# Layer 1's last sums and splits, products of zeros at the start, and one transpose for shared last tokens

## The chip, the cores and the metric

The kernel runs on one core of a Trainium2 chip. The metric is the device time of one execution in microseconds (us), lower is better. The engines are named as in the profile: PE is the matrix engine (PEld its weight loads), DVE the vector engine, ACT the scalar engine, POOL a general engine, SP the queue that issues most transfers (DMAs). Each engine works through its own instructions in order; they wait for one another by semaphores. PE writes to PSUM, which has eight banks of 512 columns in float32 per partition.

## The reference

Attention over 4 batches of 12 heads (448 tokens, 64 columns per head) with a sigmoid in the place of a softmax, then two gated layers over the 1792 tokens, each 768 to 2048 to 768, all in float32:

```python
scores = scale * np.matmul(q, k.transpose(0, 1, 3, 2)) - np.log(S)
attn = 1.0 / (1.0 + np.exp(-scores))
attn_out = np.matmul(attn, v)
...
x = np.ascontiguousarray(attn_out.transpose(0, 2, 1, 3)).reshape(B * S, H * D)
h = x @ w_in
g = h - np.tanh(h)
x = g @ w_out
...
h = x @ w_in2
r = np.maximum(h, 0.0)
g = s * (r * r) + b
out = g @ w_out2
```

## The kernel before

The two batches of a pair go through everything together: attention of 12 head pairs, layer 1, layer 2, then the next two batches (`for sb`, lines 449 to 471). A float32 product shows as two records of `MATMUL` in the trace; products of the two layers are done in three passes on split numbers (`mm3`, line 180): a high part rounded to a shorter type, and a low part that is the rest. `split` (line 186) makes them: ACT casts the high part, DVE subtracts for the low part.

**Attention.** For head pair `i`, `prep(i)` transposes queries and keys on PE into the PSUM tile `tqk`: three blocks of 128 tokens of the queries (`rawq`), three of the keys (`rawk`). The last 64 tokens of both lie together in one tile `rawr`, the queries' in one half of the partitions and the keys' in the other. Before, `rawr` is transposed twice, once beside the queries and once beside the keys, so a head pair has eight transposes. ACT copies the queries to `qt`, DVE the keys to `kt`. `qk` makes scores (`sc`, two heads side by side, two records each) and ACT the sigmoid (`af`); `av` multiplies with the values (`o`). PE's order is transposes of pair i+1, scores of chunks 2 and 3 of pair i, chunks 0 and 1 of pair i+1, then `av`. Loads of pair i+3 are issued on SP while pair i is worked on; at the start, the keys of pairs 0 and 1 go by ACT's queue (line 202).

**Layers.** `hidden` (line 296) makes 128 rows of `h` in two blocks of tokens (512 and 384 columns) and turns them into `g`. Four of these are followed by the products with `w_out`: `y` in layer 1, 24 products for each of six row blocks (`hd` 0 and 1, `d` 0 to 2), 144 in a group, four groups a layer. After a row block, `evict` (line 350) adds its two PSUM blocks to `y` on DVE; in the last group it also makes `x2`, the split input of layer 2. `bank` (line 88) hands out five single PSUM places in turn, so a block takes the place of the block five before it and waits until that was read.

**Weights.** In the first pass over the weights (sb 0) each chunk is loaded raw as float64 words (`w_load`), converted (`w_conv`: `wy` on ACT, then `wa`, `wa`, `wf` on DVE, and a store to scratch) and split (`w_split`: `whi` on ACT, `wlo` on DVE). In the second pass (sb 1) the float32 scratch is loaded, and only the split is left. `w_ahead(n)` brings loads up to n+5, conversions up to n+3 and splits up to n+2; line 372 and line 378 call it after `evict(0)` and `evict(1)`. What stands in an engine's queue is in the order in which these Python lines run.

Of the kernel before, what the change touches and what calls it, by code (L numbers as in the profile page):

```python
# [9 lines left out]
F32 = mybir.dt.float32  # L10
# [3 lines left out]
ALU = mybir.AluOpType  # L14
# [5 lines left out]
def tile_kernel(ctx, tc, q, k, v, w_in1, w_out1, w_in2, w_out2, s_in, b_in, out):  # L20
# [62 lines left out]
    def banks(name):  # L83
        return ps_p.tile([P, 2, 512], F32, tag="two", name=name, bufs=3)
# [77 lines left out]
    def upto(step, n):  # L162

        while done[step] <= n:
            yield from step(done[step]) or ()
            done[step] += 1

    def w_ahead(n, parts="ab"):

        if "a" in parts:  # L170
            yield from upto(w_load, n + 5)
            yield from upto(w_conv, n + 3)
        if "b" in parts:
            yield from upto(w_split, n + 2)

    def now(g):
        for _ in g:
# [8 lines left out]
    def split(hi, lo, t):  # L186
        act.copy(hi, t)
        dve.tensor_tensor(out=lo, in0=t, in1=hi.bitcast(F32), op=ALU.subtract)
# [4 lines left out]
    def qkv_load(i, what="qkv"):  # L193
        if i >= B * NP:
            return
        b, hs = i // NP, slice(i % NP * 2, i % NP * 2 + 2)
        if "q" in what:
            raws[i] = {"r": at_p.tile([P, 2, D], F32, tag="rawr", name="rawr", bufs=4)}
        for nm in what:
            src = {"q": q, "k": k, "v": v}[nm]  # L200

            dma = act if i < 2 and nm == "k" else sp
            rest = src[b, hs, SM:S, :].rearrange("h p d -> p h d")
            if nm == "v":
                t = at_p.tile([P, 2, NJ + 1, D], F32, tag="rawv", name="rawv", bufs=4)

                o = RM * (b % 2)
                pool.memset(t[RM - o:P - o, :, NJ, :], 0.0)
                tt, last = t[:, :, 0:NJ, :], t[o:o + RM, :, NJ, :]
                dma.dma_start(out=tt.rearrange("p e j d -> p e (j d)"), in_=src[b, hs, 0:SM, :].rearrange("h (p j) d -> p h (j d)", p=P))  # L210
            else:
                t = at_p.tile([P, NJ, 2, D], F32, tag=f"raw{nm}", name=f"raw{nm}", bufs=4)

                o = RM * ((nm == "k") ^ (b % 2))
                last = raws[i]["r"][o:o + RM]
                for e in range(2):
                    dma.dma_start(out=t[:, :, e, :], in_=src[b, hs.start + e, 0:SM, :].rearrange("(p j) d -> p j d", p=P))
            dma.dma_start(out=last, in_=rest)
            raws[i][nm] = t

    def prep(i):

        if i >= B * NP:
            return
        b = i // NP
        rq, rk, rr = (raws[i][nm] for nm in "qkr")
        both = banks("tqk")

        def transpose(ps, r, first):

            o = 0 if first else SM
            pe.transpose(ps[:, o:o + P], rr.rearrange("p h d -> p (h d)"), ident)
            for j in range(NJ):
                o = (j + first) * P
                pe.transpose(ps[:, o:o + P], r[:, j].rearrange("p h d -> p (h d)"), ident)
            return ps[:, RM:RM + S] if first else ps[:, 0:S]

        qt = at_p.tile([P, S], F32, tag="qt", name="qt", bufs=2)
        kt = at_p.tile([P, S], F32, tag="kt", name="kt", bufs=2)
        tq, tk = transpose(both[:, 0], rq, b % 2), transpose(both[:, 1], rk, 1 - b % 2)  # L240
        act.copy(qt, tq)
        dve.tensor_copy(kt, tk)
        ready[i] = qt, kt
        avs[i] = []
# [85 lines left out]
    def layer1(sb, order):  # L330
# [3 lines left out]
        for grp in range(FC // FG):  # L334
            g = [hidden(0, x, f, order if grp == 0 and f == 0 else None) for f in range(FG)]
            for hd in range(2):
# [13 lines left out]
                def evict(d):  # L350
                    dm = hd * 3 + d
                    if grp == 0:
                        y_t[dm] = x_p.tile([P, T2], F32, tag="y", name="y", bufs=7)
                    y = y_t[dm]
                    if grp == FC // FG - 1:
                        x2.append(x_p.tile([P, 2, T2], F32R, tag="x", name="x2", bufs=CC))
                    for i, ns in enumerate(BLOCKS):
                        if grp == 0:
                            act.copy(y[:, ns], ps[d, i])
                            continue  # L360
                        dve.tensor_tensor(out=y[:, ns], in0=ps[d, i], in1=y[:, ns], op=ALU.add)
                        if grp == FC // FG - 1:
                            split(x2[dm][:, 0, ns], x2[dm][:, 1, ns], y[:, ns])

                if hd == 0:

# [2 lines left out]
                else:  # L369
                    products((0,), range(FG))  # L370
                evict(0)
                now(w_ahead(pos[0] - 2))
                if hd == 0:
                    products((1,), [FG - 1])
                else:
                    products((1,), range(FG))
                evict(1)
                now(w_ahead(pos[0] - 1))
                products((2,), range(FG))
                evict(2)  # L380
        return x2
# [50 lines left out]
                        now(w_ahead(pos[0] - 2 + t // 3))  # L432


    qkv_load(0, "qk")
    qkv_load(1, "qk")
    qkv_load(0, "v")
    qkv_load(2, "qk")
    qkv_load(1, "v")
    qkv_load(2, "v")  # L440
    sp.dma_start(out=s_sb, in_=s_in.to_broadcast([P, 1]))
    sp.dma_start(out=b_sb, in_=b_in.to_broadcast([P, 1]))

    dve.memset(nlogs, NLOGS)

    act.activation(warm, nlogs, AF.Sigmoid)
# [55 lines left out]
```

## Time and profile before

| | us |
|---|---|
| median of 3 runs | 1134.53 (1134.43 to 1134.8) |
| the profiled execution | 1135.0 |
| its span | 1133.2 |
| PE busy in the span | 1119.3 |
| DVE busy | 549.1 |
| ACT busy | 489.1 |
| POOL busy | 5.4 |

PE's "busy" is time in which a matmul was under way, not time at full pace: two matmuls overlap, so pace is read from starts, or from how long a stage with a known number of products takes. PEclk is the share of the full clock of 2.4 GHz that was granted; it has two levels, 1.00 and 0.50. The clock's records begin some 14 us into the span, and the views print 1.00 ahead of that, so at the start the level is read from the matmuls' pace.

### The profile page before, as it was taken

The numbers are of one execution on the slowest core, as the hardware profiler recorded it, in microseconds if no ns is written. First come the engines' busy times: TensorE is split into PE (matmuls) and PEld (weight loads), VectorE is DVE, ScalarE is ACT, GpSimd is POOL, SyncE is SP. The second block draws the span as 40 slices with busy tenths as digits, with TensorE's granted clock in tenths as the row PEclk, the third lists the DMA queues.
The fourth block names the chain that finished last, engine by engine and source line by source line (L and its number), as shares of the span: only waits on it lengthen the run. The fifth ranks groups of instructions, "written<-read, shape, count | busy, mean of one in ns | idle before, by whom it ended". The sixth has DMA issues, their size and how long they took to land.

```text
span 1133.2 us, 14385 instructions
## 1 busy us (share of the span) xinstructions
PE 1119.3 (99%) x5760; PEld 943.6 (83%) x5760; DVE 549.1 (48%) x805; ACT 489.1 (43%) x734; POOL 5.4 (0%) x30
## 2 busy tenths in 40 slices
PE   7999999999989999999999999999999999999998
PEld 3446889898878989999954468888889899999998
DVE  0233657767677658676621123243434541534343
ACT  4774544242436664545346643331313363516060
POOL 0000000000000000000000000000000000000000
PEclk9999999999989999999999999999999999999999
DMA  5664454545444645454444202121111111111102
GB/s 133 175 177 107 156 190 140 178 156 168 145 146 134 202 140 184 138 181 153 160 121 100 77 14 70 42 70 43 56 51 47 56 56 57 57 56 56 56 14 98
DMA packets 111970, 123.62 MB, mean 109 GB/s; under 512 B 53024, under 2 KB 87328, under 8 KB 111904
## 3 DMA queue, kind: packets, MB, share of 16 engines
q1 hardware_dynamic: 110016, 122.25, 35.7%
q8 instruction: 45, 0.74, 0.3%
q10 hardware_dynamic: 1888, 0.46, 0.2%
q14 instruction: 21, 0.17, 0.1%
HBM read 92.01 MB, written 30.67 MB: 108 GB/s over the span
## 4 chain that ended last, share of the span: by engine, by line
PE 97%; DVE 2%; ACT 1%; DMA 0%; SPq 0%; issue 0%; DVEq 0%
PE h L79 41%; PE z L79 21%; PE y L79 19%; PE sc L79 7%; PE o L79 7%; PE tqk L79 2%; ACT x L79 0%; DVE y L79 0%; DVE x L79 0%; DVE wlo L79 0%; DVE wa L79 0%; DMA rawr<-in_q_dram 0%; DVE wf L79 0%; SPq L79 0%; ACT whi L79 0%
## 5 line engine op out<-in xcount | busy, mean ns | idle before, releaser
L79 PE MATMUL h<-x,whi 128*128 128x512 f32 (+1 forms) x1536 | 434.1, 363 | 0.0
L79 PEld LDWEIGHTS h<-x,whi 128*128 128x128 f32 x1536 | 283.4, 188 | 34.9 <-issue 2.7
L79 PE MATMUL h<-x,wlo 128*128 128x512 f32 (+1 forms) x768 | 279.7, 364 | 0.0
L79 PE MATMUL z<-whi,g 128*128 128x384 f32 x896 | 229.4, 334 | 0.0
L79 PE MATMUL y<-g,whi 128*128 128x512 f32 (+1 forms) x768 | 220.4, 368 | 2.0 <-ACT whi L79 1.9
L79 ACT ACTIVATE t<-h 128x512 f32<-128x512 f32 (+1 forms) x128 | 69.6, 544 | 236.5 <-PE h L79 235.9
L79 PEld LDWEIGHTS z<-whi,g 128*128 128x128 f32 x896 | 162.0, 188 | 1.3 <-issue 1.3
L79 PEld LDWEIGHTS y<-g,whi 128*128 128x128 f32 x768 | 143.8, 189 | 19.9 <-ACT whi L79 2.2
L79 PEld LDWEIGHTS h<-x,wlo 128*128 128x128 f32 x768 | 144.1, 188 | 15.2
L79 PE MATMUL z<-wlo,g 128*128 128x384 f32 x448 | 149.7, 334 | 0.0
L79 ACT CAST whi<-wf 128x768 fp32r<-128x768 f32 x128 | 106.0, 832 | 97.7 <-DVE wf L79 53.8
L79 DVE TENSOR_TENSOR wlo<-wf,whi 128x768 fp32r<-128x768 f32 x128 | 122.0, 953 | 52.9 <-ACT whi L79 52.9
L79 PE MATMUL y<-g,wlo 128*128 128x512 f32 (+1 forms) x384 | 142.2, 370 | 1.9 <-DVE wlo L79 1.7
L79 DVE TENSOR_TENSOR g<-t,g 128x512 fp32r<-128x512 f32 (+1 forms) x128 | 79.9, 624 | 83.5 <-ACT g L79 83.5
L79 ACT ACTIVATE af<-sc,nlogs 128x896 f32<-128x896 f32 x96 | 89.1, 1008 | 23.6 <-PE sc L79 13.7
L79 ACT CAST g<-t 128x512 fp32r<-128x512 f32 (+1 forms) x128 | 72.6, 567 | 33.2 <-DVE t L79 30.9
L79 PEld LDWEIGHTS z<-wlo,g 128*128 128x128 f32 x448 | 84.1, 188 | 0.0
L79 PE MATMUL sc<-qt,kt 64*128 64x448 f32 x384 | 81.3, 561 | 1.3 <-DVE kt L79 1.3
L79 PEld LDWEIGHTS y<-g,wlo 128*128 128x128 f32 x384 | 72.8, 190 | 11.7 <-DVE wlo L79 3.2
L79 DVE TENSOR_TENSOR t<-h,t 128x512 f32<-128x512 f32 x64 | 39.9, 623 | 87.7 <-ACT t L79 87.7
L79 DVE TENSOR_TENSOR z<-z 128x384 f32<-128x384 f32 x84 | 45.2, 555 | 67.5 <-PE z L79 67.5
L79 PE MATMUL o<-af,rawv 128*64 128x448 f32 x384 | 77.5, 545 | 0.0
(33 smaller groups left out, 588.5 us busy)
## 6 DMA issues: line engine op xcount, KB each, us to landing
raw<-in_moe_w_in_dram SPq DMA_DIRECT2D x32, 768.0 KB, 5.1
raw<-in_moe_w_out_dram SPq DMA_DIRECT2D x32, 768.0 KB, 4.8
win<-wf SPq DMA_DIRECT2D x32, 384.0 KB, 2.6
wout<-wf SPq DMA_DIRECT2D x32, 384.0 KB, 2.7
wf<-win SPq DMA_DIRECT2D x32, 384.0 KB, 3.0
wf<-wout SPq DMA_DIRECT2D x32, 384.0 KB, 3.1
rawq<-in_q_dram SPq DMA_DIRECT2D x48, 96.0 KB, 2.8
rawv<-in_v_dram SPq DMA_DIRECT2D x24, 192.0 KB, 2.7
```

What stands on the lines that cost most here:

```text
L79: return lambda *a, **kw: tc.keep_in_program_order(getattr(self.engine, name)(*a, **kw))
```

## The change

In `evict`, the two sums come first, then the two casts, then the two subtractions; `w_ahead` moved into `evict` (for `d` 0 and 1), with the order of its parts turned ("ba": splits ahead of conversions, after the loads), and in the last group its first step, the cast `whi`, is put between the casts and the subtractions of `x2`. At the start, DVE clears a tile `zero` and PE multiplies it with itself twice. `prep` for pairs above 0 puts queries, shared last tokens and keys side by side in one stretch of two banks, so that one transpose of `rawr` serves both, as PE's last of the pair; for pair 0 it takes two single banks and keeps both transposes of `rawr`, at the end. The keys of pair 1 are loaded by SP, and SP's first loads stand in another order.

```diff
-        if "a" in parts:
-            yield from upto(w_load, n + 5)
-            yield from upto(w_conv, n + 3)
-        if "b" in parts:
-            yield from upto(w_split, n + 2)
+        yield from upto(w_load, n + 5)
+        for part in parts:
+            if part == "a":
+                yield from upto(w_conv, n + 3)
+            else:
+                yield from upto(w_split, n + 2)
...
-            dma = act if i < 2 and nm == "k" else sp
+            dma = act if i == 0 and nm == "k" else sp
...
+        if i:
+            flat = both.rearrange("p a b -> p (a b)")
+            parts = [(flat, 0), (flat, SM + P), (flat, SM)]
+        else:
+            one = [ps_p.tile([P, 512], F32, tag="one", name="tqk0", bufs=2) for _ in range(2)]
+            parts = [(one[0], 0), (one[1], P), (one[0], SM), (one[1], 0)]
+        for (ps, o), r in zip(parts, (rk, rq) if b % 2 else (rq, rk)):
+            for j in range(NJ):
+                pe.transpose(ps[:, o + j * P:o + (j + 1) * P], r[:, j].rearrange("p h d -> p (h d)"), ident)
+        for ps, o in parts[2:]:
             pe.transpose(ps[:, o:o + P], rr.rearrange("p h d -> p (h d)"), ident)
...
-                        dve.tensor_tensor(out=y[:, ns], in0=ps[d, i], in1=y[:, ns], op=ALU.add)
-                        if grp == FC // FG - 1:
-                            split(x2[dm][:, 0, ns], x2[dm][:, 1, ns], y[:, ns])
+                        else:
+                            dve.tensor_tensor(out=y[:, ns], in0=ps[d, i], in1=y[:, ns], op=ALU.add)
+                    fill = w_ahead(pos[0] - 2 + d, "ba") if d < 2 else iter(())
+                    if grp == FC // FG - 1:
+                        for i, ns in enumerate(BLOCKS):
+                            act.copy(x2[dm][:, 0, ns], y[:, ns])
+                        next(fill, None)
+                        for i, ns in enumerate(BLOCKS):
+                            dve.tensor_tensor(out=x2[dm][:, 1, ns], in0=y[:, ns], in1=x2[dm][:, 0, ns].bitcast(F32), op=ALU.subtract)
+                    now(fill)
...
-                now(w_ahead(pos[0] - 2))
...
-                now(w_ahead(pos[0] - 1))
...
+    zero = const.tile([P, S], F32, name="zero")
+    dve.memset(zero, 0.0)
+    for _ in range(2):
+        pe.matmul(banks("none")[:, 0, :S], zero[:, :P], zero, start=True, stop=True)
```

What the change moves, at three places. DVE in sb 0, last group of layer 1, the row block `hd` 0, `d` 0 and the sums of the next one (`y` out of PSUM, `x2` the low part, `wa`, `wf` the conversion, `wlo` a weight's low part), before:

```order
L79 TENSOR_TENSOR y_1151<-y_2587,y_1151 128x512
L79 TENSOR_TENSOR x2_2633<-y_1151,x2_2633 128x512
L79 TENSOR_TENSOR y_1151<-y_2588,y_1151 128x384
L79 TENSOR_TENSOR x2_2633<-y_1151,x2_2633 128x384
L79 TENSOR_SCALAR wa_2642<-raw_2479 128x768
L79 SCALAR_TENSOR_TENSOR wa_2642<-wy_2643,wa_2642 128x768
L79 SCALAR_TENSOR_TENSOR wf_2644<-wy_2643,wa_2642 128x768
L79 TENSOR_TENSOR wlo_2652<-wf_2580,whi_2651 128x768
L79 TENSOR_TENSOR y_1175<-y_2607,y_1175 128x512
```

The same place of the changed kernel:

```order
L79 TENSOR_TENSOR y_1147<-y_2583,y_1147 128x512
L79 TENSOR_TENSOR y_1147<-y_2584,y_1147 128x384
L79 TENSOR_TENSOR x2_2629<-y_1147,x2_2629 128x512
L79 TENSOR_TENSOR x2_2629<-y_1147,x2_2629 128x384
L79 TENSOR_TENSOR wlo_2637<-wf_2576,whi_2636 128x768
L79 TENSOR_SCALAR wa_2642<-raw_2475 128x768
L79 SCALAR_TENSOR_TENSOR wa_2642<-wy_2643,wa_2642 128x768
L79 SCALAR_TENSOR_TENSOR wf_2644<-wy_2643,wa_2642 128x768
L79 TENSOR_TENSOR y_1171<-y_2603,y_1171 128x512
```

The second sum moved ahead of the first subtraction, and `wlo` ahead of the conversion of the next chunk.

PE at the start (`tqk` the transposes of a pair, `sc` scores), before:

```order
L79 MATMUL tqk_130<-ident_78,rawr_83 128x128
L79 MATMUL tqk_130<-ident_78,rawq_84 128x128 x3
L79 MATMUL tqk_130<-ident_78,rawr_83 128x128
L79 MATMUL tqk_130<-ident_78,rawk_88 128x128 x3
L79 MATMUL sc_143<-qt_131,kt_132 128x448 x2
L79 MATMUL sc_148<-qt_131,kt_132 128x448 x2
L79 MATMUL tqk_165<-ident_78,rawr_92 128x128
L79 MATMUL tqk_165<-ident_78,rawq_93 128x128 x3
L79 MATMUL tqk_165<-ident_78,rawr_92 128x128
L79 MATMUL tqk_165<-ident_78,rawk_97 128x128 x3
```

PE at the start of the changed kernel:

```order
L79 MATMUL none_126<-zero_124 128x448
L79 MATMUL none_128<-zero_124 128x448
L79 MATMUL tqk0_136<-ident_78,rawq_84 128x128 x3
L79 MATMUL tqk0_137<-ident_78,rawk_88 128x128 x3
L79 MATMUL tqk0_136<-ident_78,rawr_83 128x128
L79 MATMUL tqk0_137<-ident_78,rawr_83 128x128
L79 MATMUL sc_150<-qt_146,kt_147 128x448 x2
L79 MATMUL sc_155<-qt_146,kt_147 128x448 x2
L79 MATMUL tqk_172<-ident_78,rawq_93 128x128 x3
L79 MATMUL tqk_172<-ident_78,rawk_97 128x128 x3
L79 MATMUL tqk_172<-ident_78,rawr_92 128x128
```

Two products of zeros stand ahead, `rawr` is transposed last, and from pair 1 on once.

SP's first loads, before:

```order
L79 DMA rawq_84<-in_q_dram 128x3x64 x2
L79 DMA rawr_83<-in_q_dram 64x2x64
L79 DMA rawq_93<-in_q_dram 128x3x64 x2
L79 DMA rawr_92<-in_q_dram 64x2x64
L79 DMA rawv_101<-in_v_dram 128x2x192
L79 DMA rawv_101<-in_v_dram 64x2x64
L79 DMA rawq_106<-in_q_dram 128x3x64 x2
```

And of the changed kernel:

```order
L79 DMA rawq_84<-in_q_dram 128x3x64 x2
L79 DMA rawr_83<-in_q_dram 64x2x64
L79 DMA rawq_93<-in_q_dram 128x3x64 x2
L79 DMA rawr_92<-in_q_dram 64x2x64
L79 DMA rawk_97<-in_k_dram 128x3x64 x2
L79 DMA rawr_92<-in_k_dram 64x2x64
L79 DMA rawv_101<-in_v_dram 128x2x192
L79 DMA rawv_101<-in_v_dram 64x2x64
```

The three loads of pair 1's keys are SP's now, ahead of the values.

## Rows read from the trace of the kernel before

**Rows 1.** The page, part 1: busy us, share of the span, instructions.
```profile
PE 1119.3 (99%) x5760; PEld 943.6 (83%) x5760; DVE 549.1 (48%) x805; ACT 489.1 (43%) x734; POOL 5.4 (0%) x30
```
**Rows 2.** Windows, three y groups, tile y: length, PE, PEld, DVE, ACT, PEclk, DMA.
```profile
245.21:274.57 29.36, 29.36 (x144) 25.99 (x144) 6.09 (x11) 0.00 (x0) 1.00 0.54 171
303.64:340.37 36.73, 32.94 (x144) 27.90 (x144) 11.94 (x20) 5.66 (x10) 0.91 0.41 129
867.11:896.81 29.70, 29.62 (x144) 25.90 (x144) 11.93 (x20) 5.67 (x10) 1.00 0.13 40
```
**Rows 3.** Timeline, DVE, last y group of sb 0: start, us, instruction, [idle before].
```profile
318.86 0.68 DVE L79 TENSOR_TENSOR y<-y 128x512 f32<-128x512 f32 x1
320.23 0.69 DVE L79 TENSOR_TENSOR x<-y,x 128x512 fp32r<-128x512 f32 x1 [0.69 <-ACT x L79]
320.85 0.55 DVE L79 TENSOR_TENSOR y<-y 128x384 f32<-128x384 f32 x1
321.97 0.56 DVE L79 TENSOR_TENSOR x<-y,x 128x384 fp32r<-128x384 f32 x1 [0.58 <-ACT x L79]
...
324.97 0.95 DVE L79 TENSOR_TENSOR wlo<-wf,whi 128x768 fp32r<-128x768 f32 x1
325.84 0.69 DVE L79 TENSOR_TENSOR y<-y 128x512 f32<-128x512 f32 x1
...
329.43 0.68 DVE L79 TENSOR_TENSOR y<-y 128x512 f32<-128x512 f32 x1
```
**Rows 4.** Timeline, ACT, the same stretch.
```profile
322.65 0.81 ACT L79 CAST whi<-wf 128x768 fp32r<-128x768 f32 x1
```
**Rows 5.** Timeline, PE, the same stretch.
```profile
323.52 0.73 PE L79 MATMUL y<-g,whi 128*128 128x512 f32 x2 [1.89 <-ACT whi L79]
...
325.98 0.79 PE L79 MATMUL y<-g,wlo 128*128 128x512 f32 x1 [1.73 <-DVE wlo L79]
```
**Rows 6.** Windows of 1 us: PE, PEld, DVE, ACT, POOL, PEclk, DMA.
```profile
324.00:325.00 1.00, 0.25 (x2) 0.00 (x0) 0.96 (x3) 0.00 (x0) 0.00 (x0) 0.86 0.03 8
...
331.00:332.00 1.00, 1.00 (x5) 0.93 (x4) 0.96 (x2) 0.01 (x1) 0.00 (x0) 0.73 0.00 0
```
**Rows 7.** Timeline, PE, a head pair in the steady part of attention.
```profile
27.78 0.49 PE L79 MATMUL tqk<-ident,rawq 128*128 128x128 f32 x3
28.11 0.27 PE L79 MATMUL tqk<-ident,rawr 128*128 128x128 f32 x1
...
28.64 3.28 PE L79 MATMUL sc<-qt,kt 64*128 64x448 f32 x16
...
35.00 0.33 PE L79 MATMUL tqk<-ident,rawr 128*128 128x128 f32 x1
```
**Rows 8.** Timeline, PE, the start.
```profile
5.26 0.45 PE L79 MATMUL tqk<-ident,rawr 128*128 128x128 f32 x1 [5.26 <-DMA rawr<-in_q_dram]
...
6.14 0.42 PE L79 MATMUL tqk<-ident,rawr 128*128 128x128 f32 x1
...
8.48 3.36 PE L79 MATMUL sc<-qt,kt 64*128 64x448 f32 x8 [1.28 <-DVE kt L79]
...
13.66 3.47 PE L79 MATMUL sc<-qt,kt 64*128 64x448 f32 x16
...
20.22 0.33 PE L79 MATMUL tqk<-ident,rawr 128*128 128x128 f32 x1
```
**Rows 9.** Timeline, DVE, the start.
```profile
0.81 0.06 DVE L79 MEMSET nlogs<- 128x1 f32 x1 [0.81 <-PEq L486]
7.80 0.62 DVE L79 COPY kt<-tqk 128x448 f32<-128x448 f32 x1 [6.93 <-ACT qt L79]
```
**Rows 10.** Timeline, SP's queue, the start: when it issues.
```profile
0.74 1.59 SPq L79 DMA_DIRECT2D rawq<-in_q_dram  x2
...
3.05 1.29 SPq L79 DMA_DIRECT2D rawq<-in_q_dram  x2
```
**Rows 11.** DMA issues up to 16 us: KB each, median us to landing.
```profile
rawq<-in_q_dram SPq DMA_DIRECT2D x8, 96.0 KB, 3.0
```

More of the change, by code (lines that the diff above doesn't have):

```diff
@@ L226, in prep @@
         rq, rk, rr = (raws[i][nm] for nm in "qkr")
-        both = banks("tqk")
-        def transpose(ps, r, first):
-            o = 0 if first else SM
+        both = banks("tqk") if i else None
+        if i:
[8 more added lines that the diff above has]
+        for ps, o in parts[2:]:
             pe.transpose(ps[:, o:o + P], rr.rearrange("p h d -> p (h d)"), ident)
[L233 to L236, printed above, removed]
+        tq, tk = (flat[:, 0:S], flat[:, S:2 * S]) if i else (one[0][:, 0:S], one[1][:, RM:P + SM])
+        if b % 2:
+            tq, tk = tk, tq
         qt = at_p.tile([P, S], F32, tag="qt", name="qt", bufs=2)
         kt = at_p.tile([P, S], F32, tag="kt", name="kt", bufs=2)
-        tq, tk = transpose(both[:, 0], rq, b % 2), transpose(both[:, 1], rk, 1 - b % 2)
         act.copy(qt, tq)
@@ L359, in evict @@
                             act.copy(y[:, ns], ps[d, i])
-                            continue
-                        dve.tensor_tensor(out=y[:, ns], in0=ps[d, i], in1=y[:, ns], op=ALU.add)
-                        if grp == FC // FG - 1:
-                            split(x2[dm][:, 0, ns], x2[dm][:, 1, ns], y[:, ns])
+                        else:
[8 more added lines that the diff above has]
+                    now(fill)
                 if hd == 0:
@@ L432, in layer2 @@
                         now(w_ahead(pos[0] - 2 + t // 3))
[L435 to L440, printed above, removed]
+    for i, what in ((0, "qk"), (1, "qk"), (0, "v"), (1, "v"), (2, "qkv")):
+        qkv_load(i, what)
     sp.dma_start(out=s_sb, in_=s_in.to_broadcast([P, 1]))
     sp.dma_start(out=b_sb, in_=b_in.to_broadcast([P, 1]))
+    zero = const.tile([P, S], F32, name="zero")
+    dve.memset(zero, 0.0)
+    for _ in range(2):
+        pe.matmul(banks("none")[:, 0, :S], zero[:, :P], zero, start=True, stop=True)
     dve.memset(nlogs, NLOGS)
```

## The prediction, as it was put on record

> **What bounds the kernel now.** I read the page first: PE is busy for 99% of the span and DVE for 48% [rows 1], so what is worth something is either PE work taken out, or PE time that is spent waiting or at half clock. The busy share hides the second, so I next laid PE's starts in a row by stage and looked for stages with the same products and another length. All stages of a kind agree within 0.05 us, with four exceptions, and the change touches three: the start, and the last group of y products in layer 1 in either pass over the weights. The fourth, the end of the span, stays as it is. A group of 144 y products takes 29.36 us where nothing waits; the last one of sb 0 takes 36.73, at a mean clock of 0.91, the last one of sb 1 29.70 [rows 2]. That is 7.37 and 0.34 us to be had.
>
> Why sb 0's is long is seen on DVE. Per row block it adds the first block, waits 0.69 us for ACT's cast of it, subtracts, adds the second, waits 0.58, subtracts, then converts and splits a chunk of weights [rows 3]. From one such step to the next it is 325.84 - 318.86 = 6.98 us; a step without weights is 329.43 - 325.84 = 3.59 [rows 3]. PE makes a row block in 29.36 / 6 = 4.89. DVE's steps are longer than PE's, four of six hold weights, and a weight's low part is the last thing in a step. PE stood for 1.89 us for a `whi`, which ACT began at 322.65 [rows 4], and for 1.73 for its `wlo` [rows 5]. After that the granted clock fell from 1.00 to 0.50 (2.4 to 1.2 GHz): the share of 0.86 in the microsecond from 324 puts the fall at 324.7, that of 0.73 from 331 the rise at 331.5 [rows 6]. From 326.0 on PE worked 5.5 us at half pace, so 2.7 of the 7.37 us are the clock's, and 4.6 to 4.7 are waits.
>
> **Term 1: one transpose less.** In the steady part three transposes are followed by the next after 28.11 - 27.78 = 0.33 us [rows 7], 0.11 each. 23 pairs lose one; pair 1's is counted with the start, so 22 x 0.11 = 2.4 us. It is on the path, as PE works through a pair without a gap: ACT and DVE are done with copies and sigmoids earlier, and their order within a pair is the same. Nothing else is late next: SP needs less than a pair's time for a pair's eight issues at 0.65 each [rows 10], 5.2 of about 7.3 us. Bounds: 1.9 (if the switch from `rawr` to another tile costs what it cost before) and 2.6.
>
> The Trainium skill, page TensorE: Matmul & The Clock Gate, Part 4: PE-mode transpose, gives about 275 ns for a transpose of 128 x 128 in a kernel. By it this term would be an estimated 22 x 0.275 = 6 us. The trace speaks against it: the busy time of one record is near that figure, but starts are 0.11 apart, and the stream's length goes by starts.
>
> **Term 2: the last group of layer 1.** In the new order the second sum no longer stands behind the first subtraction. In a step that begins at 0, by the durations of [rows 3]: sums at 0 and 0.62; ACT casts from 0.73 to 1.35 and on to about 1.8; DVE subtracts at 1.4 and 2.0; `wlo` needs ACT's `whi`, about 1.75 to 2.55, and starts at 2.6 for 0.95; the conversion, three operations, takes the rest. Of the two waits (0.69 + 0.58 = 1.27) some 0.3 is left, so a step is 1.0 us shorter: 5.95 with weights, about 2.5 without. `wlo` is ready 3.5 us into a step where it was at 6.98. DVE's first sum of the group comes 8.2 us in (7 of 24 stretches of 1.22, less the last half); its steps then end at 14.2, 20.1, 22.6, 28.5, 34.4 and 36.9. PE would need the second `wlo` of the second half at 17.6 (12 stretches for the first half, 2 more, and the high passes) and gets it at 17.7: 0.1 to 0.5 of a wait. The second block of the fifth row block takes the place of the first block of the third, which is read at 20.1 to 20.8, and PE is there at 20.1 to 20.4: 0.4 to 0.7. And layer 2's first `h` wants the last low part at 36.4 and gets it at 36.5 to 36.9: 0.15 to 0.4. Together 0.65, up to 1.5. None is near the 1.7 us waits ahead of which the clock fell; the 0.34 us in sb 1's group left it at 1.00 [rows 2]. So 7.37 - 0.65 = 6.7 us, bounds 5.4 and 7.3. What is late next is DVE still, as 5.95 stands against 4.89. The conversion comes later within a step, which nobody waits for soon: its `wf` is split one step later. In groups 0 to 2 the turned order moves nothing on PE, since they had no waits to lose. `whi` waits for PE to be done with the weights four back; those are the ones of the half before, read to the end some 4.9 us earlier, so ACT isn't held.
>
> In sb 1 steps with weights have no conversion; the wait of 0.34 us is for a `wlo` that now comes earlier. I take all of it: 0.3, bounds 0 and 0.34.
>
> **Term 3: the start.** PE begins at 5.26 and its first scores at 8.48; the transposes are 0.22 apart ((6.14 - 5.26) / 4), twice the steady 0.11, and eight score records are busy for 3.36 us, where sixteen take 3.28 later: half clock, although the view prints 1.00 there. The 16 score records from 13.66 run mostly at full pace, so the clock rose near 14.1 [rows 7, 8]. What the change does, in order. (a) DVE clears `zero` from 0.81 on. The trace has no such memset; a memset of one column is 0.06 and a copy of 448 columns out of PSUM 0.62 [rows 9], so 0.06 to 0.62, and I take 0.35. (b) The first scores, eight records, are two chunks of two heads side by side and are busy for 3.36 at half clock [rows 8], so a chunk is 1.5 to 1.7. A zero product needs all rows of the array for the same 448 columns, so it takes as long as a chunk, and both 3.0 to 3.4: from 1.2 to about 4.3. That is ahead of the data: the second query load is issued about 1.5 and lands 3.0 later, at 4.5 [rows 10, 11]. So the products hide in PE's wait; were the memset 0.6 longer, they would begin to delay. (c) Queries come first, keys next, `rawr` last, so PE can begin at about 4.6 rather than 5.26. (d) Eight transposes at half pace take 1.76, and the copies of pair 0 no longer follow each other: DVE's waited for ACT's [rows 9], and now both read banks of their own, which saves one copy of 0.5 to 0.6. Scores then start at 4.6 + 1.76 + 0.2 + 0.62 + 0.06 = 7.25, 1.2 us earlier. (e) The clock. It rose 5.6 us after the first score (8.48 to 14.1), and 5.5 us after work went on at 326.0 [rows 5, 6]. Counted from 1.2 that would be 6.8, before the scores, with everything from 7.25 on at full pace: eight score records 1.6, seven transposes 0.9, sixteen records 3.2, and the values' products 3.16 (35.00 - 28.64 - 3.2, [rows 7]) make 8.9, where 20.22 - 8.48 = 11.74 stand now. That is 2.85 (pair 1's transpose in it), 4.05 with (d). At full pace ACT's two sigmoids and a copy between the first scores and pair 1's `kt` have little room, and I leave 0.3 to 0.4 for that: 3.7. Ends: a rise at 14.1 as before leaves the earlier start and the transpose, 1.4; a rise ahead of the transposes gives another 0.85, 4.9.
>
> (f) Three loads move from ACT's queue to SP's and stand ahead of the values. They are SP's seventh to ninth issue, 0.65 each [rows 10], so the last goes out near 6.2 and lands by 9.2; pair 1's last transposes come at 7.25 + 1.6 + 0.65 = 9.5. Cover 0.3 us; without it up to 0.5 is lost, and that is in the bounds. The Trainium skill (its first page, Trainium Kernel Development and Optimization, Key Constraints) says that several issuing engines only save sequencer time, since they share 16 DMA engines. By that the move costs three issues on SP, an estimated 2 us for all that is queued behind; by the rows pair 2's last load, SP's 19th issue, goes out at 12.4, lands by 15.4 and is wanted near 16.8, so the sum stays.
>
> **Sum.** 2.4 + 6.7 + 0.3 + 3.7 = 13.1 us off. The profiled execution has 1135.0 us, 0.5 above the median of 1134.53, and 1.8 beyond its span that the change doesn't touch. Against the median: 1121.4.
>
> **Rivals.** *The clock at the start rises late.* For it: the zero products are followed by a pause until the loads land, and by another for the copies; in the trace work with pauses took 8.8 us from the first transpose to the rise. Then scores run at half pace up to about 10.5, and term 3 is 2.3 or, with no help at all, 1.4: 1122.8 to 1123.7. *DVE stays the bound in layer 1.* If a step is only 0.5 us shorter (the casts and `whi` in ACT's order hold the subtractions), PE waits 1 to 2 us twice, and the clock may fall once more for 2.7: term 2 is 2 to 4 us, 1124 to 1126. Against it: ACT's two casts and `whi` are some 2 us of a step of 6. *The change doesn't do what it says in layer 1:* the waits are for weights, and if `whi` waits as long for its `wf` as before, term 2 is 0 and the time 1128. Against it: in either order `wf` is a whole step old by then. *Slower:* the clock isn't granted in attention for long, since short waits of PE for SP's longer queue break up its work in the first pairs. A pair at half pace costs some 6 us more; 9.4 us of other gains and the 2.3 that make a difference as well as the 1.4 of the earlier start are eaten when the rise comes later than about 14 + 2 x 13 = 40 us, four pairs in: 1136.8 there, 1139.8 at 46. Against it: one transpose less makes no pause, and SP gains 2 us on PE in each pair.
>
> **How the numbers follow.** Forecast 0.60, around 1121.4 (1119.5 to 1122.7); late clock 0.22; DVE's bound 0.11; no gain in layer 1 0.04; slower 0.02; 0.01 for a sum that comes to nothing. 0.2% is 2.3 us, about the least that a measurement of this kernel tells from none. The range from 1119.5 to 1124.3 takes in the forecast with the ends of terms 1 and 3, the late clock, and the near end of DVE's bound. Faster 0.97, same 0.01, slower 0.02.
>
> **What would show it.** Seven transposes a pair and pairs 0.11 us shorter; the last y group of sb 0 near 30 us with PEclk 1.00, no idle PE over 0.8 us, and DVE's steps near 5.95; sb 1's at 29.36; two zero products ending ahead of 4.5, scores from about 7.25 with eight records in 1.6 us, and pair 2's transposes at 16.5 rather than 20.22. It is wrong if the zero products end after the first loads, if score records are at half pace past 10 us, or if a y group of sb 0 still has a window at PEclk 0.50.

## The result, and the profile after

The changed kernel takes 1122.02 us in the median beside 1134.53; the ratio is 0.9891, 95% interval 0.9879 to 0.9904. The prediction was 1121.4 in 1119.5 to 1124.3. One of the five executions, the profiled one, took 2251.33 us: its matrix products ran at about half pace from end to end, while DVE and ACT were busy for 560 and 496 us, near the usual 549 and 488, and it is left out of the ratio. What follows is read from another execution of the same program (`e1_after`, 1122.69 us median, ratio 0.9891 again, 0.9877 to 0.9904), whose span is 1120.9 us beside 1133.2 before.

The page, part 1 (busy us, share of the span, instructions), answers to [rows 1]:

```profile
PE 1114.8 (99%) x5741; PEld 939.0 (84%) x5741; DVE 549.1 (49%) x806; ACT 487.6 (44%) x734; POOL 5.4 (0%) x30
```

PE has 19 instructions fewer: 23 transposes taken out and four records of the two products of zeros put in. It is 4.5 us less busy, though 12.3 us are gone: most of the gain was idle time, or busy time at half clock that the shares don't show as loss.

**Layer 1.** Windows over three y groups, tile y (columns as in [rows 2]):

```profile
240.88:270.24 29.36, 29.36 (x144) 25.99 (x144) 6.08 (x11) 0.00 (x0) 1.00 0.53 162
299.31:329.34 30.03, 29.87 (x144) 25.86 (x144) 10.51 (x19) 4.99 (x10) 1.00 0.42 128
855.12:884.48 29.36, 29.36 (x144) 26.00 (x144) 11.89 (x21) 5.18 (x10) 1.00 0.16 44
```

The last group of sb 0 is 0.67 us longer than one that waits for nothing, where it was 7.37 longer [rows 2], and the clock of its window is 1.00. The last one of sb 1 is level. The timeline of DVE in the second of them (start, us, instruction, idle before in brackets) shows a step of the new order, which answers to [rows 3]:

```profile
313.48 1.15 DVE L79 TENSOR_TENSOR y<-y 128x512 f32<-128x512 f32 x2
314.85 1.16 DVE L79 TENSOR_TENSOR x<-y,x 128x512 fp32r<-128x512 f32 x2 [0.22 <-ACT x L79]
316.00 0.96 DVE L79 TENSOR_TENSOR wlo<-wf,whi 128x768 fp32r<-128x768 f32 x1
316.87 0.55 DVE L79 TENSOR_SCALAR wa<-raw 128x768 uint32<-128x768 uint32 x1
317.53 0.96 DVE L79 SCALAR_TENSOR_TENSOR wa<-wy,wa 128x768 uint32<-128x768 uint32 x1
318.52 0.96 DVE L79 SCALAR_TENSOR_TENSOR wf<-wy,wa 128x768 uint32<-128x768 uint32 x1
319.40 1.15 DVE L79 TENSOR_TENSOR y<-y 128x512 f32<-128x512 f32 x2
...
321.85 1.15 DVE L79 TENSOR_TENSOR y<-y 128x512 f32<-128x512 f32 x2
```

Both sums come first, both subtractions next, then the low part of a weight, then a conversion. One wait of 0.22 us for ACT is left where 0.69 and 0.58 stood. A step with weights takes 319.40 - 313.48 = 5.92 us, one without 321.85 - 319.40 = 2.45. The timeline of PE has the three places where it still stands:

```profile
317.01 0.50 PE L79 MATMUL y<-g,wlo 128*128 128x512 f32 x1
...
320.14 0.62 PE L79 MATMUL y<-g,whi 128*128 128x384 f32 x2 [0.16 <-DVE y L79]
...
335.40 0.92 PE L79 MATMUL h<-x,whi 128*128 128x512 f32 x2
```

The first begins when `wlo` (316.00 and 0.96 long) is done. Held against the starts in the group before, it and the start behind it come 0.11 and 0.10 later than the pace allows. The second waits for its bank, read by the sums of 319.40; it costs 0.31 + 0.11 = 0.42. In the third, layer 2's first `h`, the pair of records takes 0.92 instead of 0.63: it meets the low part that DVE subtracts from 335.07 on. That `h` group takes 29.38 us beside 29.09 before.

**The start.** Timeline of PE, which answers to [rows 8]:

```profile
1.39 3.35 PE L79 MATMUL none<-zero 128*128 128x448 f32 x4 [1.39 <-DVE nlogs L79]
5.02 0.87 PE L79 MATMUL tqk<-ident,rawq 128*128 128x128 f32 x3 [0.27 <-DMA rawq<-in_q_dram]
...
7.77 1.77 PE L79 MATMUL sc<-qt,kt 64*128 64x448 f32 x8 [0.81 <-DVE kt L79]
9.47 0.55 PE L79 MATMUL tqk<-ident,rawq 128*128 128x128 f32 x3
...
10.39 3.28 PE L79 MATMUL sc<-qt,kt 64*128 64x448 f32 x16
...
16.75 0.55 PE L79 MATMUL tqk<-ident,rawq 128*128 128x128 f32 x3
```

The products of zeros are over at 4.74, 0.27 us ahead of the first queries. The eight score records are busy for 1.77 us where they took 3.36, so they run at 2.4 GHz from the first on. Pair 2's transposes begin at 16.75, 3.47 us earlier than before. The timelines of DVE and ACT in the same stretch:

```profile
0.91 0.43 DVE L79 MEMSET zero<- 128x448 f32 x1 [0.91 <-PEq L499]
...
7.00 0.62 DVE L79 COPY kt<-tqk 128x448 f32<-128x448 f32 x1 [5.65 <-PE tqk L79]
```
```profile
6.78 0.53 ACT L79 COPY qt<-tqk 128x448 f32<-128x448 f32 x1 [2.51 <-PE tqk L79]
```

The copy of the keys no longer waits for ACT's, as it did in [rows 9]; the two overlap.

**A head pair in the steady part.** Timeline of PE, which answers to [rows 7]:

```profile
24.04 0.55 PE L79 MATMUL tqk<-ident,rawq 128*128 128x128 f32 x3
...
24.95 3.28 PE L79 MATMUL sc<-qt,kt 64*128 64x448 f32 x16
...
31.32 0.55 PE L79 MATMUL tqk<-ident,rawq 128*128 128x128 f32 x3
```

Seven transposes take 24.95 - 24.04 = 0.91 us from the first start to the scores, and the pair 31.32 - 24.04 = 7.28.

**The account.** By stages of PE, span against span: the start 3.47; 22 pairs with 7 transposes at 0.91 us instead of 8 at 1.02, 2.36 in all; the last y group 6.70; the `h` group behind it -0.29; sb 1's y group 0.34; one pair's scores at 54 us, 0.25 longer than before, -0.25; small ones -0.08. That is 12.25 of 12.3.

### The profile page after: what moved, and what is told of

It is laid out like the page before. It is cut to its first block, busy times and chain, and to the rows that moved or that the text cites. A ratio compares the mean times of both kernels' runs of the same rounds, so it can differ in the third digit from the quotient of the medians.

```text
span 2249.5 us, 14347 instructions
## 1 busy us (share of the span) xinstructions
PE 2243.8 (100%) x5741; PEld 1542.2 (69%) x5741; DVE 560.4 (25%) x806; ACT 495.6 (22%) x734; POOL 5.4 (0%) x30
## 4 chain that ended last, share of the span: by engine, by line
PE 100%; DVE 0%; issue 0%
PE h L79 42%; PE y L79 21%; PE z L79 21%; PE sc L79 7%; PE o L79 7%; PE tqk L79 2%; PE none L79 0%; DVE kt L79 0%; DVE z L79 0%; DVE zero L79 0%; DVE nlogs L79 0%
## 5 line engine op out<-in xcount | busy, mean ns | idle before, releaser
L79 PE MATMUL h<-x,whi 128*128 128x512 f32 (+1 forms) x1536 | 786.0, 615 | 0.0
L79 PEld LDWEIGHTS h<-x,whi 128*128 128x128 f32 x1536 | 459.0, 300 | 174.1 <-issue 150.7
L79 PE MATMUL h<-x,wlo 128*128 128x512 f32 (+1 forms) x768 | 473.8, 617 | 0.0
L79 PE MATMUL z<-whi,g 128*128 128x384 f32 x896 | 410.0, 557 | 0.0
L79 PE MATMUL y<-g,whi 128*128 128x512 f32 (+1 forms) x768 | 393.1, 615 | 0.0
L79 PEld LDWEIGHTS z<-whi,g 128*128 128x128 f32 x896 | 269.7, 302 | 50.0 <-issue 34.8
L79 PEld LDWEIGHTS h<-x,wlo 128*128 128x128 f32 x768 | 230.0, 299 | 84.4 <-issue 73.6
L79 PEld LDWEIGHTS y<-g,whi 128*128 128x128 f32 x768 | 228.8, 298 | 85.4 <-issue 68.7
L79 PE MATMUL z<-wlo,g 128*128 128x384 f32 x448 | 249.5, 557 | 0.0
L79 PE MATMUL y<-g,wlo 128*128 128x512 f32 (+1 forms) x384 | 236.5, 616 | 0.0
```

The costliest lines, as they stand in the source:

```text
L79: return lambda *a, **kw: tc.keep_in_program_order(getattr(self.engine, name)(*a, **kw))
```

## The experiments

Each time below is given beside runs of the kernel before on the same chip; "gain" is the difference of the two medians. The changed kernel itself gained 12.5.

> The changed kernel once more, for its stages. My theory (three separate gains): about 1122.0 us; last y group of sb 0 near 30.0 us (29.4 to 30.9) with PEclk 1.00 throughout, that of sb 1 at 29.36; a steady head pair 7.28 us where it was 7.39; pair 2's transposes at 16 to 17 us. Rival 'the clock at the start rises late': pair 2's transposes at 17.8 us or later. Rival 'DVE stays the bound in layer 1': last y group of sb 0 at 31 to 33 us, and then the start must have given more than I said.

Measured 1122.69 (1122.04 to 1122.69); the stages are read above.

**Without the products of zeros** (`e2_no_zeros`):

```diff
-    zero = const.tile([P, S], F32, name="zero")
-    dve.memset(zero, 0.0)
-    for _ in range(2):
-        pe.matmul(banks("none")[:, 0, :S], zero[:, :P], zero, start=True, stop=True)
```

> The changed kernel without the cleared tile and its two products; nothing else is changed. My theory (the products bring the clock up early): the clock rises near 14 us as before, so 2.0 to 2.7 us slower than the changed kernel, about 1124.4. Rival 'products of zeros bring nothing, the start gains by its order and its separate banks alone': within 0.3 us of the changed kernel, 1122.0.

Measured 1125.46 (1124.91 to 1126.21), gain 9.7: by the medians the products are worth 2.8 us. Timeline of PE in the profiled execution, the fastest of the four:

```profile
7.74 3.36 PE L79 MATMUL sc<-qt,kt 64*128 64x448 f32 x8 [0.81 <-DVE kt L79]
...
11.73 0.54 PE L79 MATMUL tqk<-ident,rawk 128*128 128x128 f32 x3
...
18.67 0.55 PE L79 MATMUL tqk<-ident,rawq 128*128 128x128 f32 x3
```

The scores begin as early as with them, but run at half pace, and pair 2's transposes come 1.9 us later; the span is 2.2 us longer. The transposes from 11.73 on are nearly at full pace, so the clock rose near 11.8 and not near 14, as was expected: even without the products the new order had pair 2 begin 20.22 - 18.67 = 1.55 us earlier than before the change.

**The last tokens transposed twice again** (`e3_two_rawr`), the rest of the change kept:

```diff
-            flat = both.rearrange("p a b -> p (a b)")
-            parts = [(flat, 0), (flat, SM + P), (flat, SM)]
+            one = [both[:, 0], both[:, 1]]
...
+        parts = [(one[0], 0), (one[1], P), (one[0], SM), (one[1], 0)]
```

> The changed kernel with the shared last tokens transposed twice in every pair, as pair 0 does it. My theory (0.107 us each): 23 x 0.107 = 2.5 us slower, 1124.5. By the page's 275 ns a transpose: 6.3 us slower, 1128.3. If a transpose were hidden: 1122.0.

Measured 1124.95 (1124.44 to 1126.73), gain 10.2, so 2.3 us for the 23 transposes, 0.10 each. A pair in the steady part, timeline of PE:

```profile
23.58 0.55 PE L79 MATMUL tqk<-ident,rawq 128*128 128x128 f32 x3
...
24.29 0.38 PE L79 MATMUL tqk<-ident,rawr 128*128 128x128 f32 x2
24.61 3.28 PE L79 MATMUL sc<-qt,kt 64*128 64x448 f32 x16
```

Eight transposes take 24.61 - 23.58 = 1.03 us from the first start to the scores.

**Layer 1's last sums as before** (`e4_old_evict`): `evict` and the order of conversion and split are those of the kernel before, attention and start those of the changed one.

```diff
-                    if grp == FC // FG - 1:
-                        for i, ns in enumerate(BLOCKS):
-                            act.copy(x2[dm][:, 0, ns], y[:, ns])
...
+                        if grp == FC // FG - 1:
+                            split(x2[dm][:, 0, ns], x2[dm][:, 1, ns], y[:, ns])
...
+                now(w_ahead(pos[0] - 2))
```

> The changed kernel with evict and w_ahead as they were before (sums, casts and subtractions block by block, conversions ahead of splits). My theory: 6.5 to 7.2 us slower, about 1129.0, with the last y group of sb 0 back at about 36.7 us and a stretch at PEclk 0.50, and that of sb 1 at 29.7. Rival 'DVE stays the bound': only 3 to 5 us slower, 1125 to 1127.

Measured 1129.8 (1129.29 to 1129.92), gain 5.4: 7.1 us of the change lie here, and the rival that saw no gain in layer 1 falls. Windows, tile y, over the group and over a stretch of it:

```profile
299.29:336.38 37.09, 32.95 (x144) 27.93 (x144) 11.94 (x20) 5.66 (x10) 0.91 0.42 130
...
321.00:327.00 6.00, 5.02 (x13) 4.40 (x14) 3.21 (x6) 1.75 (x3) 0.50 0.66 199
```

The group is about as long as in [rows 2] (36.73), and the clock is at 1.2 GHz for at least these 6 us of it.

**Sums first, but conversions ahead of splits** (`e5_sums_ab`), and **block by block as before, but splits ahead of conversions** (`e6_blocks_ba`): each half of the new order alone.

```diff
-                    fill = w_ahead(pos[0] - 2 + d, "ba") if d < 2 else iter(())
+                    fill = w_ahead(pos[0] - 2 + d, "ab") if d < 2 else iter(())
```

> The changed kernel with the parts of w_ahead in evict as before (conversions ahead of splits), sums still ahead of the splits of x2. My theory (PE waited for two things: banks that a late sum held, and a low part of weights that stood at the end of a step): DVE's steps stay near 5.95 us, but the second weights of the second half are ready 6 us into a step and not 3.5, so PE waits some 0.3 us for whi and 2.1 for wlo; the last y group of sb 0 is 31.8 us, or up to 34 if the clock falls again; 1.7 to 4 us slower than the changed kernel, 1124.4 to 1126.7. Rival 'the order of the sums alone does it': last y group near 30.0, 1122.7.

> The other half: sums, casts and subtractions block by block as before, splits of weights ahead of conversions. My theory (DVE's step stays near 7 us, and it is the chain of six steps that sets when layer 2 can begin): low parts are earlier, so PE's waits for weights in the last y group are 2 to 3 us rather than 4.6, but layer 2's first h waits 4 to 5 us for the last x2; y group 32 to 33 us and the first h group of layer 2 33 to 34 where it is 29.1; together 6 to 8 us slower than the changed kernel, 1129 to 1131, whether or not the clock falls. Rival 'the low parts alone do it': near the changed kernel, 1122.7 to 1124.

`e5_sums_ab` measured 1126.97 (1125.85 to 1128.01), gain 7.8; `e6_blocks_ba` 1132.44 (1131.39 to 1134.27), gain 2.4. The waits of PE in the first (us in total, times, longest) and the window over its last y group, tile y:

```profile
PE y L79 <- DVE wlo L79: 2.3, 1, 2.3
```
```profile
299.22:333.08 33.86, 31.45 (x144) 27.12 (x144) 11.59 (x20) 5.27 (x10) 0.95 0.45 140
```

With the conversion in front, the low part is 2.3 us late once, and the clock falls once more. In the second, the waits of PE and the windows over its y group and the `h` group behind it (with POOL ahead of PEclk):

```profile
PE h L79 <- ACT x L79: 3.2, 1, 3.2
```
```profile
298.71:331.39 32.68, 30.44 (x146) 25.88 (x145) 21.95 (x32) 10.99 (x17) 0.00 (x0) 1.00 0.36 109
331.39:367.08 35.69, 32.52 (x146) 27.54 (x145) 27.09 (x39) 20.88 (x33) 0.00 (x0) 0.90 0.51 164
```

Here the y group has lost 4.4 us against `e4_old_evict` and no longer sees the clock fall; but the steps of DVE are still too long, so the last of them is late for layer 2, PE waits 3.2 us for `x`, and the clock falls there; the `h` group is 6.6 us longer. Group and `h` group together take 59.4 us in the changed kernel, 62.9 with sums alone, 68.4 with splits alone, and 66.2 with neither. Splits ahead are worth 3.5 us behind the shorter steps; alone they cost 2.2. These are lengths of one execution each; the medians have the same order: 4.7, 10.1 and 7.1 us behind the changed kernel.

**The kernel before with the products of zeros alone** (`e7_before_zeros`):

```diff
+    zero = const.tile([P, S], F32, name="zero")
+    dve.memset(zero, 0.0)
+    for _ in range(2):
+        pe.matmul(banks("none")[:, 0, :S], zero[:, :P], zero, start=True, stop=True)
```

> The kernel before with only the cleared tile and its two products added. My theory (the products count as work for the clock, whatever follows): the clock rises by some 4 to 5 us earlier, 2.0 to 2.8 us faster than the kernel before, 1132.4 to 1133.0 beside 1135.0. Rival (they help only together with the new order of the start, since the old one leaves PE idle too long before the scores): less than 1 us faster.

Measured 1135.0 (1132.09 to 1135.62) beside 1134.79, ratio 0.9999 (0.9989 to 1.0009): no gain in the median, so the theory that these products are worth the same wherever they stand falls. The ten executions spread from 1132.09 to 1135.62; the profiled one, 1134.04, is among the faster. Timeline of PE and windows (with POOL) of its start:

```profile
6.24 0.49 PE L79 MATMUL tqk<-ident,rawk 128*128 128x128 f32 x3
8.28 3.22 PE L79 MATMUL sc<-qt,kt 64*128 64x448 f32 x8 [1.55 <-DVE kt L79]
...
19.01 0.33 PE L79 MATMUL tqk<-ident,rawr 128*128 128x128 f32 x1
```
```profile
8.00:9.00 1.00, 0.72 (x2) 0.37 (x4) 0.22 (x1) 0.00 (x0) 0.00 (x0) 0.73 0.50 130
9.00:11.00 2.00, 2.00 (x8) 0.69 (x4) 0.00 (x0) 0.95 (x1) 0.00 (x0) 0.50 0.51 116
11.00:12.00 1.00, 1.00 (x5) 0.57 (x4) 0.00 (x0) 0.52 (x2) 0.00 (x0) 0.56 0.64 145
```

The clock did rise: the transposes are at full pace, three in 0.49 us. Then PE stood 1.55 us for the two copies, one behind the other, and the share of 0.73 puts a fall near 8.5, just as the scores began. They ran at half pace, and the clock came back near 11.9. Pair 2 still began 20.22 - 19.01 = 1.21 us earlier than before, so this execution kept part of the gain; the slower ones left no trace.

**Pair 1's keys on ACT's queue again** (`e8_keys_act`):

```diff
-            dma = act if i == 0 and nm == "k" else sp
+            dma = act if i < 2 and nm == "k" else sp
```

> The changed kernel with the keys of pair 1 loaded by ACT's queue again. My theory (nobody waits for these loads in either place): within 0.3 us of the changed kernel, 1122.7, pair 0's transposes begin at about 5.0 to 5.3 us. Rival 'SP's longer queue costs': 0.3 to 0.8 us faster, 1122.1. Rival 'loads of pair 1 on two queues take the DMA engines from pair 0's, or ACT's copy of the queries waits for its issues': 0.3 to 0.8 us slower, 1123.3.

Measured 1122.36 (1121.99 to 1124.07), gain 12.4: PE waits for these loads on neither queue. The traces do differ in one place, one head pair's scores at 54 us. Timelines of PE and ACT, `e1_after` first, then this run:

```profile
54.07 3.53 PE L79 MATMUL sc<-qt,kt 64*128 64x448 f32 x16
54.58 0.53 ACT L79 COPY qt<-tqk 128x448 f32<-128x448 f32 x1 [0.77 <-PE tqk L79]
```
```profile
54.25 3.28 PE L79 MATMUL sc<-qt,kt 64*128 64x448 f32 x16
54.41 0.53 ACT L79 COPY qt<-tqk 128x448 f32<-128x448 f32 x1 [0.43 <-PE tqk L79]
```

With the keys on ACT's queue ACT's copy of the queries comes sooner behind the transposes, and the scores are 0.25 us shorter. In this execution the first queries landed 0.18 us later (the transposes begin at 5.20), so the whole does not show it.

**A conversion moved one row block later** (`e9_conv_late`), to remove what is left of the waits:

```diff
-                    fill = w_ahead(pos[0] - 2 + d, "ba") if d < 2 else iter(())
+                    fill = w_ahead(pos[0] - 2 + min(d, 1), ("ba", "b", "a")[d])
...
-                        next(fill, None)
+                        if d < 2:
+                            next(fill, None)
```

> The changed kernel, but the conversion and the loads that were ACT's fill at d = 1 of a y group are given at d = 2; d = 0 and the splits on DVE stay. In the changed kernel the last y group of layer 1 takes 30.03 us and the h group behind it 29.38, against 29.36 and 29.08 for the same groups where nothing waits: 0.67 + 0.30 = 0.97 us of waits are left there. Theory one (ACT's conversion at d = 1 stands ahead of its copies of the next sums, these come late to the subtractions, and so to the banks and to the weights' split): the two groups come down to 29.4 to 29.5 and 29.1, the whole is 0.6 to 0.95 us faster than the changed kernel, 1121.1 to 1122.1. Theory two (DVE's own queue of three sums, split and subtractions sets it, whatever ACT does): both groups stay, the time is that of the changed kernel within 0.2 us.

Measured 1121.7 (1121.23 to 1122.16), gain 13.3, ratio 0.9883 (0.987 to 0.9897). Window over its last y group, tile y:

```profile
299.26:328.85 29.59, 29.59 (x144) 25.91 (x144) 10.38 (x18) 4.55 (x9) 1.00 0.41 124
```

The bank wait is gone, 0.21 us for `wlo` are left, and the `h` group behind takes 29.09. The two groups are 0.73 us shorter than in the changed kernel, so this is the fastest version by its median; the whole agrees in size (0.8 by the gains), but the intervals overlap, so the whole doesn't prove it. Theory one has the size right and probably the engine wrong. The edit moves the conversion's three DVE operations as well as ACT's one, and ACT had been idle for over 3 us ahead of its casts; so it is likely DVE's queue, which the next sums now leave earlier; no run moved the operations of one engine alone.

**The start alone on the kernel before** (`e10_start_alone`): the products of zeros, two banks of one for pair 0, and the new order of the loads; the last tokens transposed twice, sums as before.

```diff
+            one = [ps_p.tile([P, 512], F32, tag="one", name="tqk0", bufs=2) for _ in range(2)]
+        parts = [(one[0], 0), (one[1], P), (one[0], SM), (one[1], 0)]
...
+    for i, what in ((0, "qk"), (1, "qk"), (0, "v"), (1, "v"), (2, "qkv")):
+        qkv_load(i, what)
```

> The kernel before with the change's start alone: products of zeros, pair 0's queries and keys in two banks of one (two copies side by side), loads of pair 1 all by SP and ahead of pair 2's; every pair transposes its last tokens twice, and layer 1's last sums are as before. The products alone gained nothing (1135.0 beside 1134.8), the new order of the start without them 2.8 us less than all of it. Theory one (the products pay only where the scores follow the transposes soon, since the clock falls back in a longer pause of TensorE): 2.5 to 3.5 us faster than before, 1131.3 to 1132.3; scores begin at 7.1 to 8.0, pair 2's transposes at 16.2 to 17.0, and the clock is not lower again ahead of the attention's end. Theory two (what the start gains is spent in the attention on loads or copies that the other parts of the change relieve): under 1 us faster, over 1133.8.

Measured 1132.04, gain 3.0, ratio 0.9976 (0.9967 to 0.9985). Ten of eleven executions lie in 1131.38 to 1132.31, one took 1135.41; that one was profiled, and its timeline of PE shows what it lacks:

```profile
5.44 0.88 PE L79 MATMUL tqk<-ident,rawq 128*128 128x128 f32 x3 [0.69 <-DMA rawq<-in_q_dram]
...
8.19 3.35 PE L79 MATMUL sc<-qt,kt 64*128 64x448 f32 x8 [0.81 <-DVE kt L79]
...
20.22 0.55 PE L79 MATMUL tqk<-ident,rawq 128*128 128x128 f32 x3
```

The queries landed 0.4 us later than in `e1_after`, the transposes and scores ran at half pace, and pair 2 came no earlier than before the change. This is the late clock of the rival, 3.4 us above the median of the other ten. Of 31 executions with the whole new start and both products (the changed kernel's eight undisturbed ones, `e3_two_rawr`, `e8_keys_act`, `e9_conv_late` and this), four were 2.0 to 3.4 us above the median of the others of their kernel; that the other three have the same cause is likely, but they left no trace. `e4_old_evict`, with the same start, has five more and none that stands out; `e5_sums_ab` and `e6_blocks_ba` are not counted, since clock falls in the layers may spread their times too.

**The pause filled** (`e11_bridge`): `e7_before_zeros` with two more products of zeros behind pair 0's transposes.

```diff
+        if i == 0:
+            for _ in range(2):
+                pe.matmul(banks("none")[:, 0, :S], zero[:, :P], zero, start=True, stop=True)
         act.copy(qt, tq)
```

> The kernel before with the two products of zeros ahead of pair 0's transposes, as in the run that gained nothing, and two more behind these transposes, where TensorE stood idle from 6.7 to 8.28 us and the clock, up at 5.05, was lower again from 8.46 to 11.87. Theory one (the pause is what let the clock fall): with the pause filled the clock stays up, the two more take 1.7 us at full clock, the scores begin at 8.3 to 8.5 and take 1.7 us where they took 3.22, pair 2's transposes begin at 17.2 to 17.8 (19.01 with the pause, 20.22 before), and the whole is 1.5 to 2.5 us faster than before, 1132.3 to 1133.3. Theory two (the clock's fall there has another cause than the pause): it falls again at some 8.5, the two more cost up to 1.7 us of delay, and the whole is 1134.8 to 1136.

Measured 1134.2 beside 1135.02, ratio 0.9988 (0.9979 to 0.9997), between the two theories. Single executions stand apart: five of eleven took 1132.15 to 1132.6, about what theory one has, and six 1134.2 to 1135.11, five of them as theory two has it. The profiled one is the fastest of the six:

```profile
5.71 0.45 PE L79 MATMUL tqk<-ident,rawr 128*128 128x128 f32 x1 [0.97 <-DMA rawr<-in_q_dram]
...
7.45 2.72 PE L79 MATMUL none<-zero 128*128 128x448 f32 x4
10.10 1.77 PE L79 MATMUL sc<-qt,kt 64*128 64x448 f32 x8
```

Here the transposes found half clock, the added products took 2.72 us instead of 1.7, and from the scores on all was at full pace. So here the clock rose only within the filled pause and then stayed up; it does not test a fall behind an earlier rise, and the five fast executions left no trace. Without the added products one of ten executions was under 1133, with them five of eleven. That the pause lets the clock fall is therefore likely, but not shown.

**One product of zeros in place of two** (`e12_one_zero`):

```diff
-    for _ in range(2):
+    for _ in range(1):
```

> The changed kernel with one product of zeros in place of two: TensorE is busy from 1.39 to 3.07 us, and idle to the first transposes at 5.0. Theory one (work ahead of a pause doesn't hold the clock, as the run of products ahead of the old start showed): the clock rises as without products, at 10 to 12 us, and most of their 2.8 us is lost, 1124.5 to 1125.5. Theory two (any work ahead of the transposes counts): the clock is up at 7 to 8.5, and at most 0.8 us is lost, 1122.0 to 1123.2.

Measured 1124.63 (1124.31 to 1124.88), gain 10.4: 2.1 of the 2.8 us are lost. Timeline of PE:

```profile
5.42 0.87 PE L79 MATMUL tqk<-ident,rawq 128*128 128x128 f32 x3 [2.17 <-DMA rawq<-in_q_dram]
...
8.17 3.36 PE L79 MATMUL sc<-qt,kt 64*128 64x448 f32 x8 [0.81 <-DVE kt L79]
```

After 2.17 us of idle time the transposes and scores are at half pace, as without any product ahead of them. The edit halves the work and makes the pause longer at once, so it can't tell which of the two counts.

## Why the prediction was right, and where not

The terms add up as far as it was tested: the start alone gained 3.0, the start with the transposes 5.4, all of it 12.5, so the transposes are worth 2.4 behind the start and, taken out of the whole, 2.3. Layer 1's part was not run alone.

**Term 1** held: 2.4 forecast, 2.36 by the stages (22 x 0.107), 2.3 by `e3_two_rawr` (with pair 1's). The Trainium skill, page TensorE: Matmul & The Clock Gate, Part 4: PE-mode transpose, would have made it an estimated 6 us with its 275 ns a transpose (stated there for bf16); the trace disagrees, since what counts in this stream is the distance of starts, 0.107 us.

**Term 2** held in mechanism and nearly in size. DVE's steps are 5.92 and 2.45 us where 5.95 and 2.5 were laid out, no window is below full clock, and the three waits that were to be left are the three that are left: 0.21 for `wlo` (0.1 to 0.5), 0.42 for the bank (0.4 to 0.7), 0.29 for layer 2's first `h` (0.15 to 0.4). They make 0.92 (0.96 by the length of the two groups), not the 0.65 that was entered, so the term is 6.4 rather than 6.7. The forecast counted on a `wlo` ready 3.5 us into a step instead of 6.98, but gave the turned order of conversion and split no share of its own: `e5_sums_ab` shows that it carries 3.5 us of the term, and `e6_blocks_ba` that without the shorter steps it does harm, at layer 2's first products, where the forecast had looked for 0.15 to 0.4 only. Sb 1's 0.34 came in full.

**Term 3** came out at 3.47 for 3.7, by errors that nearly cancel. The transposes began at 5.02, not 4.6: the first queries landed later than the median transfer of [rows 11] said. The copies cost 0.1 more. So the scores came at 7.77 instead of 7.25. From there to pair 2 it took 8.98 us, where 8.9 and 0.35 of reserve were entered. The memset took 0.43 from 0.91 on (0.35 from 0.81 entered); that moved the products to 1.39, with no harm, since 0.27 us of cover were left.

The step that failed in part is (e). It counted the clock from the first product of zeros on, as if pauses behind it did not matter, and left pauses to a rival. The runs speak for its doubt: the same products gained nothing ahead of the old start, where the clock fell again behind a pause of 1.55 us (`e7_before_zeros`), and one alone, 2.17 us ahead of the transposes, gained 0.7 us of the 2.8 (`e12_one_zero`, where the work was halved as well). The products pay together with the new order that brings the scores forward. By the medians 2.8 us hang on both; in the two traces it is 1.92 of the term's 3.47 us, and the other 1.55 came without the products. The late clock had a chance of 0.22; among the undisturbed executions of kernels with the whole start, four of 31 look like it. What sets the moment of the rise from one execution to the next stays open: with the same start it rose before the transposes in `e3_two_rawr` (its scores start at 7.10), behind them, between 6.97 and 7.77, in `e1_after`, and in the profiled execution of `e10_start_alone` only near 14.3, by the pace of its score records. So that (e)'s 6.8 came near `e1_after` is in part luck of that execution. A third, shorter product that reaches up to the first queries was not tried.

**Loads.** (f) put no cost on the three loads that went to SP, with a cover of 0.3 us; `e8_keys_act` agrees as to waits for them, and its time can't be told from the changed kernel's (1122.36 and 1122.69). The Trainium skill, Trainium Kernel Development and Optimization, Key Constraints, has it that queues share their DMA engines and a second one saves only the issuing: the times don't speak against it, but as nobody waits for these loads, no run here shows it.

One loss was in no term: 0.25 us in one pair's scores at 54 us. It goes with the choice of queue: all nine traced versions in which SP loads pair 1's keys have it, `e10_start_alone` among them, and the four in which ACT does (the kernel before, `e7_before_zeros`, `e11_bridge`, `e8_keys_act`) do not. There ACT's copy of the queries follows the transposes 0.3 us later than elsewhere; how the queue does that, so long after the loads, stays open.

## What to carry to other kernels

Where one engine feeds another in steps, write down its queue with durations and compare the step with the consumer's pace; order the step so that round trips to a third engine overlap, and put what is wanted soonest first, but only once the steps are short enough, since the queue's last item else moves the wait to the next stage. Products made only to bring the clock up paid here in most executions with pauses of 0.27 and 0.81 us behind them, and not in the median with 0.91 and 1.55; so look at the pauses behind them as part of the same change. Look at single executions beside the median: a gain that hangs on the moment of a clock's rise comes and goes from run to run.

## What the runs showed of the hardware

- The clock can fall again right after its first rise: in `e7_before_zeros` it was up for the transposes, down at 0.50 from 9 to 11 us, and up after 12, with 1.55 us of idle PE ahead of the fall.
- Clock falls in layer 1 differed in length: a mean of 0.91 over 37.09 us is 6.7 us at half clock in `e4_old_evict`, with two waits of some 2 us, and 0.95 over 33.86 is 3.4 us in `e5_sums_ab`, with one of 2.3.
